# Four DMA transposes of the first tile of chunks 2 and 3 issued ahead of the output stores in a fused attention and GEGLU kernel

## The chip, the cores and the metric

One core of one Trainium2 chip. Times are device microseconds (us) of an execution, given as medians of several. Ratios with a 95% interval compare a kernel with the kernel before in runs that were interleaved on the same chip. The profile's span is some 1.7 us shorter than the time of the same execution (227.4 us of 229.07 us for the kernel before).

## The reference

The input x has 2048 rows of 512 bf16 values. It is normalized, goes through an attention branch and a gated feed-forward branch, and the product of both is added to x:

```python
xn = _layernorm(x, axis=-1)
s = _A_ref(xn, A_wqkv, A_wo)     # 32 heads of 16; each row sees 8 rows, 2 apart; softmax; output projection
g = _silu(_B_ref(xn, B_w_gate, B_w_up, B_w_down))   # (gelu(xn @ w_gate) * (xn @ w_up)) @ w_down, 1792 wide
return x + s * g
```

## The kernel before

The rows are worked on in four chunks of 512 (TQ), each of four tiles of 128 rows (TPQ = 4). For each chunk TensorE does 14 steps of the gate and up projections ("glu"), the QKV projection of the next chunk ("qkv"), the down projection ("down"), the attention sums, and the output projection ("finish"). All of these need the normalized rows transposed, with the 512 features on the partitions. For tiles 6 and 7 of chunk 1 and all of chunks 2 and 3 the transposition is a DMA, four per tile, issued from SyncE's queue, which also issues every other transfer:

```python
    def transpose_by_dma(t, cs=range(NC)):
        j, i = divmod(t, TPQ)
        if i == 0 and 0 in cs:
            xnT[j] = xtp.tile([P, NC, TQ], BF16, name="xnT")      # two buffers
        for c in cs:
            nc.sync.dma_start(
                out=xnT[j][:, c, i * P : (i + 1) * P],
                in_=xns[t][:, c * P : (c + 1) * P],
                transpose=True,
            )

    def project(ps, w, lo, j, i0=0, n=TQ):                        # glu and qkv
        for dk in range(NC):
            nc.tensor.matmul(ps, lhsT=w[:, dk, lo : lo + P],
                rhs=xnT[j][:, dk, i0 : i0 + n], start=(dk == 0), stop=(dk == NC - 1))

    # ... load_v: four loads of v_arr, 520 KB each; sums() ends with load_v(j + 1)

    def finish(j, tt, cols, sl):
        # ... four matmuls into s
        m = sm2.tile([P, n], BF16, name="m")
        nc.vector.tensor_tensor(out=m[:], in0=s[:], in1=sl[:], op=ALU.mult)
        o_t = sm4.tile([P, n], BF16, name="o_t")                  # four buffers
        nc.vector.tensor_tensor(out=o_t[:], in0=m[:], in1=x_sb[:, t, cols], op=ALU.add)
        nc.sync.dma_start(out=out2d[t * P : (t + 1) * P, cols], in_=o_t[:])
```

The order of the program is the order of issue on each engine. Side work is hung on steps of the main loop with `at`, and `run` calls it ahead of the step:

```python
    for i in range(TPQ):
        # ...
        at(("down", 0, 2), normalize, 2 * TPQ + i)
        at(("glu", 1, 0), transpose_by_dma, 2 * TPQ + i)
        # ...
        at(("qkv", 2, i), normalize, 3 * TPQ + i)
        at(("glu", 2, 0), transpose_by_dma, 3 * TPQ + i)
    # ...
    for j in range(NJ):
        for fc in range(NF):
            run("glu", j, fc)
            glu(j, fc)
        if j + 1 < NJ:
            for i, fo in enumerate((0, 1, 4, 5, 2, 3, 6, 7, 8, 9, 10, 11)):
                run("qkv", j + 1, i)
                qkv(j + 1, fo)
            full = slice(0, D)
            sl = []
            for tt in range(TPQ):
                run("down", j, tt)
                sl.append(down(j, tt, full))
                if tt == 0:
                    sums(j)
            divide(j)
            for tt in range(TPQ):
                finish(j, tt, full, sl[tt])
```

So chunk 2's 16 transposes are issued at the start of chunk 1's loop, behind chunk 0's four output stores, and are first read by the QKV projection at the end of that loop; chunk 3's likewise, one chunk later. Chunks are counted from 0.

The softmax here doesn't subtract the row's maximum and nothing guards it: scores larger than these inputs give would overflow.

## Time and profile before

| | before |
|---|---|
| median of the runs at the time of the prediction | 229.31 us (228.83 to 229.8) |
| span of the profile | 227.4 us |
| TensorE busy | 222.3 us (98%) |
| last transpose of chunk 2 issued / first QKV matmul that reads chunk 2 | 96.11 / 98.37 us |
| last transpose of chunk 3 issued / first QKV matmul that reads chunk 3 | 150.16 / 152.23 us |

In the profile PE is TensorE, PEld its loading of weights, DVE VectorE, ACT ScalarE, POOL GpSimd, and SPq the queue from which SyncE issues DMAs. The granted clock is TensorE's clock as the chip allowed it, as a share of full speed. A line of the timeline has a start, a length (both in us), an engine, a source line, an operation with its output and input, and how often it came in a row. The length of a DMA instruction is that of its issue alone. The lines themselves are in the prediction below.

### The profile page before, as it was taken

What the parts mean: (1) busy time and instruction counts of PE and PEld (TensorE: products, weight loads), DVE (VectorE), ACT (ScalarE), POOL (GpSimd) and SP (SyncE); (2) the same over time, 40 slices, a digit from 0 to 9 for tenths busy, and PEclk for the clock granted to TensorE, in tenths of its full rate; (3) what the DMA queues carried; (4) which work ended last, traced back from release to release, by engine and by line L of the source; (5) the groups of instructions that cost most, each with busy time, mean ns of one, the idle gap of its engine ahead of it and who ended that gap; (6) DMA issues with size and microseconds to landing.
All of it is one profiled execution on the core that took longest, in us unless ns stands there. A gap on an engine that the chain in (4) does not pass through costs nothing.

```text
span 227.4 us, 3595 instructions
## 1 busy us (share of the span) xinstructions
PE 222.3 (98%) x1326; PEld 107.1 (47%) x1326; DVE 151.8 (67%) x278; ACT 132.2 (58%) x209; POOL 25.0 (11%) x67
## 2 busy tenths in 40 slices
PE   8999999999999999999999999999999999999993
PEld 4785444444444444444444444444444444444453
DVE  4696981899995588969904759924934348971434
ACT  4279769777531676766751466767763356756210
POOL 1027901000040000333700000000000000000000
PEclk9999999999999999999999999999999999999998
DMA  6999499941039911100219921100217950000011
GB/s 206 349 395 384 127 201 142 321 109 67 28 83 202 223 25 25 29 10 0 92 33 206 214 71 29 26 18 0 81 26 151 197 140 0 0 0 22 12 37 56
DMA packets 30130, 24.64 MB, mean 108 GB/s; under 512 B 10784, under 2 KB 29600, under 8 KB 30112
## 3 DMA queue, kind: packets, MB, share of 16 engines
q1 hardware_dynamic: 30112, 24.41, 44.3%
q8 instruction: 10, 0.16, 0.3%
q14 instruction: 8, 0.07, 0.1%
HBM read 18.74 MB, written 4.34 MB: 102 GB/s over the span
## 4 chain that ended last, share of the span: by engine, by line
PE 95%; DVE 1%; ACT 1%; DMA 1%; issue 0%; DVEq 0%
PE y_ps L443 21%; PE u_ps L249 21%; PE g_ps L249 21%; PE qkv_ps L249 16%; PE s_ps L459 6%; PE L_ps L338 3%; PE o_ps L406 3%; PE qk_ps L554 2%; DMA x_sb<-in_A_x_dram 1%; PE v_ps L554 1%; ACT L431 1%; DVE stats L182 1%; PE tr L214 1%; PE den_ps L358 0%; ACT ge L431 0%; ACT vst L273 0%
## 5 line engine op out<-in xcount | busy, mean ns | idle before, releaser
L249 PE MATMUL u_ps<-xnT,wu_sb 128*128 128x512 bf16 x224 | 57.5, 379 | 0.0
L249 PE MATMUL g_ps<-xnT,wg_sb 128*128 128x512 bf16 x224 | 57.5, 379 | 0.0
L443 PE MATMUL y_ps<-wd_sb,h 128*128 128x512 bf16 (+1 forms) x238 | 49.9, 367 | 0.0
L435 DVE TENSOR_TENSOR h<-ge,u 128x512 bf16<-128x512 bf16 x56 | 23.8, 425 | 30.7 <-ACT u L433 29.0
L433 ACT ACTIVATE u<-u_ps 128x512 bf16<-128x512 f32 x56 | 33.5, 598 | 16.4 <-PE u_ps L249 16.4
L431 ACT ACTIVATE ge<-g_ps 128x512 bf16<-128x512 f32 x56 | 33.5, 598 | 16.2 <-PE g_ps L249 16.0
L320 DVE TENSOR_TENSOR pk<-q_sb,k_sb 128x1024 bf16<-128x1024 bf16 (+1 forms) x56 | 38.9, 762 | 4.6 <-ACT k_sb L273 4.6
L392 DVE TENSOR_TENSOR pv<-E,v_arr 128x1024 bf16<-128x1024 bf16 (+1 forms) x48 | 39.8, 863 | 0.2 <-issue 0.2
L249 PE MATMUL qkv_ps<-xnT,wqkv_sb 128*128 128x512 bf16 (+1 forms) x192 | 37.0, 352 | 0.0
L443 PEld LDWEIGHTS <-h 128*128 128x128 bf16 x238 | 23.0, 98 | 25.9 <-issue 1.3
L249 PEld LDWEIGHTS <-wu_sb 128*128 128x128 bf16 x224 | 21.9, 98 | 26.6 <-issue 0.3
L249 PEld LDWEIGHTS <-wg_sb 128*128 128x128 bf16 x224 | 21.7, 98 | 26.3 <-issue 0.8
L451 ACT ACTIVATE sl<-y_ps 128x512 bf16<-128x512 f32 (+1 forms) x17 | 9.7, 572 | 32.6 <-PE y_ps L443 32.6
L249 PEld LDWEIGHTS <-wqkv_sb 128*128 128x128 bf16 x192 | 18.8, 98 | 17.5
L467 DVE TENSOR_TENSOR m<-s_ps,sl 128x512 bf16<-128x512 f32 (+1 forms) x17 | 11.1, 655 | 17.0 <-PE s_ps L459 17.0
L418 DVE TENSOR_TENSOR oT<-o_ps,rb 128x1024 bf16<-128x1024 f32 x8 | 9.4, 1220 | 13.8 <-DMA rb<-rs_d 13.8
L199 POOL TENSOR_TENSOR rstd<-rstd,mhalf 128x1 f32<-128x1 f32 x12 | 8.0, 663 | 69.9 <-DVE rstd L196 69.9
L459 PE MATMUL s_ps<-wo_sb,oT 128*128 128x512 bf16 (+1 forms) x68 | 14.8, 366 | 0.0
L273 ACT ACTIVATE vst<-qkv_ps 128x512 bf16<-128x512 f32 x14 | 8.4, 597 | 3.7 <-PE qkv_ps L249 3.7
L273 ACT ACTIVATE k_sb<-qkv_ps 128x512 bf16<-128x512 f32 x14 | 8.4, 601 | 3.2 <-PE qkv_ps L249 3.2
L273 ACT ACTIVATE q_sb<-qkv_ps 128x512 bf16<-128x512 f32 x14 | 8.3, 603 | 3.0 <-PE qkv_ps L249 3.0
L459 PEld LDWEIGHTS <-oT 128*128 128x128 bf16 x68 | 6.7, 98 | 7.2
(57 smaller groups left out, 131.4 us busy)
## 6 DMA issues: line engine op xcount, KB each, us to landing
v_arr<-vT SPq DMA_DIRECT2D x16, 520.0 KB, 8.5
vT<-vst SPq DMA_DIRECT2D x8, 256.0 KB, 2.2
out_dram<-o_t SPq DMA_DIRECT2D x15, 128.0 KB, 3.4
wg_sb<-in_B_w_gate_dram SPq DMA_DIRECT2D x2, 896.0 KB, 10.1
wu_sb<-in_B_w_up_dram SPq DMA_DIRECT2D x2, 896.0 KB, 11.0
wd_sb<-in_B_w_down_dram SPq DMA_DIRECT2D x1, 1792.0 KB, 11.5
wqkv_sb<-in_A_wqkv_dram SPq DMA_DIRECT2D x4, 384.0 KB, 4.9
x_sb<-in_A_x_dram SPq DMA_DIRECT2D x3, 512.0 KB, 10.5
```

Source lines behind the costliest of these rows:

```text
L249: nc.tensor.matmul(ps, lhsT=w[:, dk, lo : lo + P], rhs=xnT[j][:, dk, i0 : i0 + n], start=(dk == 0), stop=(dk == NC - 1),)
L273: nc.scalar.activation(out=dst, in_=ps, func=AF.Copy)
L320: nc.vector.tensor_tensor(out=st[j]["pk"][w][:, c0 : c0 + n, :], in0=st[j]["q"][:, c0 : c0 + n, :], in1=k_sb[j][:, c0 : c0 + n, off : off ...
L392: nc.vector.tensor_tensor(out=pv[:, d : d + n, :], in0=st[j]["E"][:, wh, :].unsqueeze(1).to_broadcast([P, n, TQ]), in1=st[j]["va"][:, 4 * ...
L418: nc.vector.tensor_tensor(out=oT[:, g : g + 2, :], in0=st[j]["o"][:, g : g + 2, :], in1=st[j]["rb"][:].unsqueeze(1).to_broadcast([P, 2, TQ ...
L431: nc.scalar.activation(out=ge[:], in_=g_ps[:], func=AF.Gelu_apprx_tanh)
L433: nc.scalar.activation(out=u[:], in_=u_ps[:], func=AF.Copy)
L435: nc.vector.tensor_tensor(out=h[:], in0=ge[:], in1=u[:], op=ALU.mult)
L443: nc.tensor.matmul(y[:], lhsT=st[j][fc][:, tt * P : (tt + 1) * P], rhs=wd_sb[:, fc, cols], start=(fc == 0), stop=(fc == NF - 1),)
L451: nc.scalar.activation(out=sl[:], in_=y[:], func=AF.Silu)
L459: nc.tensor.matmul(s[:], lhsT=st[j]["oT"][:, g, tt * P : (tt + 1) * P], rhs=wo_sb[:, g, cols], start=(g == 0), stop=(g == NC - 1),)
L467: nc.vector.tensor_tensor(out=m[:], in0=s[:], in1=sl[:], op=ALU.mult)
```

## The change

SyncE has nothing to issue for five to six microseconds at the end of chunks 0 and 1, while it waits for the first output tile. The change puts the four transposes of the next-but-one chunk's first tile there:

```diff
-        at(("glu", 1, 0), transpose_by_dma, 2 * TPQ + i)
+        at(("glu", 1, 0) if i else ("down", 0, 3), transpose_by_dma, 2 * TPQ + i)
         at(("glu", 1, 10 + i), moments, 3 * TPQ + i)
         at(("qkv", 2, i), normalize, 3 * TPQ + i)
-        at(("glu", 2, 0), transpose_by_dma, 3 * TPQ + i)
+        at(("glu", 2, 0) if i else ("down", 1, 3), transpose_by_dma, 3 * TPQ + i)
```

## The prediction

> **What bounds the kernel now.** I read the page first (busy shares, then the chain that ended last), then the waits of TensorE, then the waits and the timeline of the DMA queue that SyncE feeds, and last a window of three microseconds around the place where the moved transposes are used.
>
> The page of the kernel before, its busy shares and the engines of its chain:
>
> ```profile
> span 227.4 us, 3595 instructions
> PE 222.3 (98%) x1326; PEld 107.1 (47%) x1326; DVE 151.8 (67%) x278; ACT 132.2 (58%) x209; POOL 25.0 (11%) x67
> ...
> PE 95%; DVE 1%; ACT 1%; DMA 1%; issue 0%; DVEq 0%
> ```
>
> TensorE is busy for 222.3 of 227.4 us, and 95% of the chain is TensorE. The chain in order of time has no piece of another engine between 20.93 us (first matmuls of the feed-forward loop) and 223.91 us (the end): 203 us of matmuls laid end to end. The waits of TensorE agree; this is the whole answer for that engine:
>
> ```profile
> PE warm_ps L231 <- PEq L622: 0.8, 1, 0.8
> PE v_ps L554 <- DVE xnT L225: 0.5, 1, 0.5
> ```
>
> Both lie in the first 7 us. The columns are total wait, times, longest. No matmul waits for a DMA transpose anywhere. Over 74.4 to 98.4, 98.4 to 128.2, 128.2 to 152.2 and 152.2 to 182.1 us, the four stretches that hold the transposes and their first use, the busy time of TensorE equals the length of the stretch (107.70 of 107.70 us) at a granted clock of 1.00. So there is nothing to take away from TensorE's idle time in the stages that the change touches.
>
> The diff touches only the order of SyncE's DMA issues. Its timeline around the ends of chunks 0 and 1 (start, length, line, operation, count):
>
> ```profile
> 65.37 2.64 SPq L294 DMA_DIRECT2D v_arr<-vT  x4
> 73.05 3.52 SPq L470 DMA_DIRECT2D out_dram<-o_t  x4
> 76.62 3.86 SPq L241 DMA_TRANSPOSE xnT<-xn  x3
> ```
>
> ```profile
> 117.97 2.58 SPq L294 DMA_DIRECT2D v_arr<-vT  x4
> 126.91 3.52 SPq L470 DMA_DIRECT2D out_dram<-o_t  x4
> 130.48 20.91 SPq L241 DMA_TRANSPOSE xnT<-xn  x16
> ```
>
> SyncE has nothing to issue from 68.0 to 73.05 us and from 120.55 to 126.91 us: its next instruction is an output store, and the waits of that queue put the longest single waits in these two windows (5.0 and 6.3 us) down to the store's operand o_t from VectorE. Then the stores and all 16 transposes go out, and the last transpose comes late. The timeline between 96.5 and 99.9 us:
>
> ```profile
> 96.11 1.23 SPq L241 DMA_TRANSPOSE xnT<-xn  x1
> ...
> 98.15 1.82 PEld L249 LDWEIGHTS <-wqkv_sb 128*128 128x128 bf16 x9
> 98.37 1.89 PE L249 MATMUL qkv_ps<-xnT,wqkv_sb 128*128 128x512 bf16 x8
> ```
>
> The last of chunk 2's 16 transposes is issued at 96.11 us. From issue to landing a transpose takes 2.3 us in that window (2.2 at least, 4.0 at most, the 4.0 being the first, behind other traffic), so it lands at about 98.4 us. It carries the fourth quarter of the contraction, which the fourth matmul of the first QKV group reads, at 98.37 + 3 x 0.216 = 99.02 us (0.216 is 0.86 us for four matmuls in the chain in order of time). **The slack is about 0.6 us.** For chunk 3 the last issue is at 150.16 us (130.48 + 20.91 - 1.23), landing is near 152.5 us, the first QKV matmul starts at 152.23 us and the fourth at 152.88: slack about 0.4 us. That is narrow, but it is positive in the trace, and this is what the change enlarges.
>
> **What the Trainium skill says.** "Perfetto Trace Analysis", section "DMA Instruction — HWDGE", says that the profiled length of such an instruction ends when the sequencer is free again and leaves out the data movement, and that a semaphore wait lies ahead of its start. The trace agrees: a transpose is 1.23 us long and lands 2.3 us after its start; the idle stretch ahead of the stores is such a wait. "DMA: Bandwidth & Descriptors", section "Rules for kernel authors", advises issuing a DMA early and waiting on it late, which is the intent here, and says a transpose next to ordinary DMAs needs nothing; the order of the changed kernel has indeed no new wait between the kinds except a reused semaphore (below). The same page, section "Queues, rings and completion order", says that each DMA engine takes descriptors in ring order. From this I expect the early transposes to land behind the four v_arr loads that are in flight, not beside them; the 4.0 us of the first transpose at 76.62 us, behind stores that land at 80.4 us, agrees. "Perfetto Trace Analysis", section "Identifying the Most-Contended Engine", warns that matmul busy time says little of the distance from roofline. That holds here too, but the change does not make a matmul shorter.
>
> **The change part by part.** The order of instructions of both kernels differs on SyncE alone; TensorE, VectorE, ScalarE and GpSimd keep theirs. Nothing is added or removed: 4 of 16 transposes of chunk 2, and 4 of chunk 3, go from after the chunk's four output stores to before them.
>
> 1. *What they need is there.* The four normalizes of chunk 2 run on VectorE from 65.85 to 67.22 us, before the load of v_arr has been issued. Those of chunk 3 come at about 100 us. The buffer of xnT that is overwritten was last read at 44.6 and 98.4 us.
>
> 2. *Where they go.* Four transposes at 1.23 to 1.3 us are 4.9 to 5.2 us. They fit almost exactly into 68.0 to 73.05 (5.05 us) and easily into 120.55 to 126.91 (6.36 us). So chunk 2's run from 68.05 to about 73.2, chunk 3's from 120.6 to about 125.7 us, and no first store is late by more than 0.2 us.
>
> 3. *What comes of the stores.* The DMA semaphores go round by eight. In the kernel before, the transposes behind the stores reused those of the four v_arr loads; now the stores do, so store n waits for v_arr load n to land. From the median landing times of windows that hold one or two issues each: chunk 1's loads land at about 70.8, 73.6, 76.2 and 79.1 us (issue plus 5.4, 7.6, 9.6, 11.8), chunk 2's at 123.2, 125.8, 128.4 and 131.0. The stores were issued at 73.05, 74.11, 75.17, 76.24 and at 126.91, 127.97, 129.04, 130.10. So in chunk 0 the third is delayed by some 1.0 us and the fourth by 2.9, in chunk 1 only the fourth, by 0.9. Nobody reads what is stored, and o_t has four buffers whose next use is one chunk (54 us) later: this delay costs nothing.
>
> 4. *What comes of the last transpose.* Chunk 2: the fourth store ends at about 79.5 us, then 12 transposes at 1.25 to 1.3 us take 15.3 us: issue is over at about 95 instead of 97.34 us. Chunk 3: from 131.4 us, over at about 146.8 instead of 151.39. So of the 5.0 us moved, some 2.4 and 4.6 us come off the last landing. The slack grows from 0.6 to about 3 us and from 0.4 to about 5 us.
>
> 5. *What lies on the path.* TensorE's first use is at 98.37 and 152.23 us whatever the transposes do, since it comes right behind the last feed-forward matmul. Taken off the path: 0.00 us in the profiled run. In runs whose DMA is half a microsecond slower, TensorE may stall for a few tenths, twice. The three runs of before lie 228.83 to 229.8 us, so all such effects together are within 1 us; I give the change 0.1 us on average. Sum: 229.31 - 0.1 = 229.2 us.
>
> **The rivals.**
> - *A hidden stall in the unprofiled runs.* If TensorE usually lost about half a microsecond at both chunk borders, the gain would be up to 1.0 us, near 228.3 us. For it: slacks of 0.4 and 0.6 us are thin. Against it: the profiled run took 229.07 us, in the middle of the others, and shows no stall. Even then the gain is 0.4%.
> - *The load of v_arr is slowed by the early transposes.* The first product with v_arr is at 80.61 us and the load lands at 79.1: 1.5 us of room (134.47 against 131.0 in the next chunk). Transposes are 32 KB each, 0.13 MB, which at the 190 GB/s of that window are 0.7 us if they went ahead; behind in the ring they cost none. If they took 3 us, VectorE would slip by 1.5 us, but the last h of the chunk is ready at 99.7 us and used first at 108.7 us, so TensorE would not see it. Time: 229.2 us.
> - *SyncE gets stuck.* If a transpose ahead of the stores waited long (for instance for a semaphore of the rb loads that it now reuses), stores and 12 transposes would slip with it, and each microsecond beyond the slack stalls TensorE. Those loads of 32 KB land in 1.8 us and are needed by the divide at 67.14 and 119.30 us, so they are done. If the fourth store had to wait until 82 us, the twelve would end at 97.3, as now. A loss would need more than that: with 2 us in one chunk 231 us. I give it a few per cent.
> - *The end of the kernel.* The last stores are not moved; nothing changes there.
>
> **How the range and the chances follow.** The work of TensorE is untouched, 203 us without a gap, and the change can win only gaps. Range: the spread of before (228.83 to 229.8), widened by 0.5 us downwards for the first rival and 0.2 us upwards: 228.3 to 230.0 us. Faster by over 2% means below 224.7 us, which would need 4.6 us from gaps that do not exist; slower by over 2% means above 233.9 us and needs a stall of 4 us that nothing points to. One per cent each.
>
> **What the changed profile would show.** TensorE's waits unchanged, still two, in the first 7 us; its start of QKV at 98.4 and 152.2 us unchanged. SyncE's timeline: four transposes at 68 and 120.6 us ahead of the stores, 12 behind, the last issued near 94 and 145.5 us. Waits of the stores with a DMA of v_arr as the releaser for the last one or two stores of chunk 0: that shows step 3. If the twelve still end near 97 us, step 4 is wrong, and the idle time was not there to be had. The prediction as a whole would be wrong if a matmul waited for xnT in the changed kernel, or if the time moved by over 1 us with the same gapless TensorE.

## The result, and the profile after

The kernel after took 228.95 us (median of 6 runs, 228.81 to 229.35), the kernel before 229.41 us in the same rounds (228.83 to 229.8). The ratio is 0.9986 with a 95% interval of 0.9968 to 1.0003. A ratio is the mean time of one kernel's runs over that of the other's of the same rounds, so it is not quite the ratio of the medians. The class is "same".

SyncE's timeline around the ends of chunks 0 and 1, kernel after:

```profile
65.50 2.62 SPq L294 DMA_DIRECT2D v_arr<-vT  x4
68.22 5.08 SPq L241 DMA_TRANSPOSE xnT<-xn  x4
73.40 6.42 SPq L470 DMA_DIRECT2D out_dram<-o_t  x4
79.88 15.40 SPq L241 DMA_TRANSPOSE xnT<-xn  x12
...
118.17 2.65 SPq L294 DMA_DIRECT2D v_arr<-vT  x4
120.86 5.13 SPq L241 DMA_TRANSPOSE xnT<-xn  x4
127.04 5.01 SPq L470 DMA_DIRECT2D out_dram<-o_t  x4
132.10 15.98 SPq L241 DMA_TRANSPOSE xnT<-xn  x12
```

The four transposes fill the idle time, as intended. The stores behind them now take 6.42 and 5.01 us to go out instead of 3.52. The queue's own waits, kernel after, say what for (the queue and line that waited, the releaser, then total us, times, longest); first 60 to 90 us, then 115 to 140 us:

```profile
SPq L470 <- DMA v_arr<-vT: 4.4, 2, 2.5
...
SPq L470 <- DMA v_arr<-vT: 2.4, 2, 2.2
```

Two stores in each place wait for a v_arr load to land. A wait counts from the end of the instruction before, so it is not the delay of the store. The delay is read from the start of the fourth store in each place:

```profile
79.49 0.33 SPq L470 DMA_DIRECT2D out_dram<-o_t  x1
...
131.72 0.33 SPq L470 DMA_DIRECT2D out_dram<-o_t  x1
```

These are 3.25 and 1.62 us later than in the kernel before (76.24 and 130.10 us), and each comes right after the landing of the fourth v_arr load, at 79.4 us (67.44 + 12.0) and 131.6 us (120.13 + 11.5). The last transpose is issued 1.23 us ahead of the end of its row, so at 94.05 us instead of 96.11, and at 146.85 us instead of 150.16. TensorE takes no notice. Its waits in the kernel after, all of them:

```profile
PE warm_ps L231 <- PEq L622: 0.8, 1, 0.8
PE v_ps L554 <- DVE xnT L225: 0.5, 1, 0.5
```

They are the two of before, number for number. The chain in order of time shows where the 0.1 us between the two spans (227.4 and 227.5 us) lies; its QKV pieces are first those of the kernel before, then those of the kernel after:

```profile
12.61 5.25 PE qkv_ps L249 x48
44.62 10.36 PE qkv_ps L249 x48
98.53 10.36 PE qkv_ps L249 x48
152.39 10.36 PE qkv_ps L249 x48
```

```profile
12.75 5.25 PE qkv_ps L249 x48
44.76 10.36 PE qkv_ps L249 x48
98.66 10.36 PE qkv_ps L249 x48
152.52 10.36 PE qkv_ps L249 x48
```

The kernel after is 0.14 us later at the first of these pieces, before anything that the change touches, and 0.13 us later at the last. From the first piece to the end of the span it is 214.79 us before (227.4 - 12.61) and 214.75 us after (227.5 - 12.75).

### The profile page after: what moved, and what is told of

It is laid out like the page before. It is cut to its first block, busy times and chain, and to the rows that moved or that the text cites. A ratio compares the mean times of both kernels' runs of the same rounds, so it can differ in the third digit from the quotient of the medians.

```text
span 227.5 us, 3601 instructions
## 1 busy us (share of the span) xinstructions
PE 222.6 (98%) x1326; PEld 107.6 (47%) x1326; DVE 151.6 (67%) x278; ACT 132.1 (58%) x209; POOL 18.9 (8%) x67
## 4 chain that ended last, share of the span: by engine, by line
PE 97%; ACT 1%; DVE 0%; issue 0%; DVEq 0%
PE y_ps L443 21%; PE u_ps L249 21%; PE g_ps L249 21%; PE qkv_ps L249 16%; PE s_ps L459 6%; PE L_ps L338 3%; PE o_ps L406 3%; PE qk_ps L554 2%; PE warm_ps L231 1%; PE v_ps L554 1%; PE qk_ps L529 1%; ACT L431 1%; PE tr L214 1%; PE den_ps L358 0%; PE v_ps L529 0%; ACT ge L431 0%
## 6 DMA issues: line engine op xcount, KB each, us to landing
wd_sb<-in_B_w_down_dram SPq DMA_DIRECT2D x1, 1792.0 KB, 11.6
```

## The experiments

Ten kernels were run, in three calls, each call on one chip with its own runs of the kernel before. All ten gave correct results.

| kernel | median us | before, same call | ratio | 95% interval |
|---|---|---|---|---|
| a_again: the change once more | 229.29 | 229.25 | 1.0002 | 0.9983 to 1.0021 |
| c2_only: chunk 2 alone | 229.44 | 229.04 | 1.0011 | 0.9996 to 1.0026 |
| c3_only: chunk 3 alone | 229.27 | 229.04 | 1.0010 | 0.9991 to 1.0030 |
| all16: all 16 transposes first | 229.12 | 229.04 | 1.0005 | 0.9989 to 1.0020 |
| b_extra1: before, one redundant transpose per chunk | 231.40 | 229.24 | 1.0094 | 1.0075 to 1.0114 |
| b_extra2: before, two | 234.00 | 229.25 | 1.0201 | 1.0177 to 1.0225 |
| b_extra4: before, four | 243.34 | 229.04 | 1.0621 | 1.0604 to 1.0637 |
| a_extra2: after, two | 229.09 | 229.25 | 0.9994 | 0.9975 to 1.0012 |
| a_extra4: after, four | 233.54 | 229.25 | 1.0183 | 1.0154 to 1.0213 |
| all16_extra4: all 16 first, four | 229.32 | 229.24 | 1.0000 | 0.9984 to 1.0016 |

### Is there a gain at all? The change again, and each half

a_again is the changed kernel unaltered. The halves each keep one of the two changed lines:

```diff
 c2_only
-        at(("glu", 1, 0), transpose_by_dma, 2 * TPQ + i)
+        at(("glu", 1, 0) if i else ("down", 0, 3), transpose_by_dma, 2 * TPQ + i)
 c3_only
-        at(("glu", 2, 0), transpose_by_dma, 3 * TPQ + i)
+        at(("glu", 2, 0) if i else ("down", 1, 3), transpose_by_dma, 3 * TPQ + i)
```

> The changed kernel once more, in five rounds, to narrow the interval of its ratio to the kernel before. Theory (TensorE is gapless at both places in both kernels, nothing to win): ratio 1.000 within 0.15%. Rival (the kernel before loses up to 0.5 us at each of two chunk borders in runs that were not profiled): ratio 0.996 to 0.998 with an interval that leaves out 1.

> The change for chunk 2 alone. Theory (no gain anywhere): ratio 1.000. Rival (a small true gain at each border): ratio 0.999, half of the change's.

> The change for chunk 3 alone, whose slack is the smaller one (0.4 us). Theory (no gain anywhere): ratio 1.000. Rival (a small true gain at each border, the larger where the slack is smaller): ratio 0.998 to 0.999.

None of the three differs from the kernel before; the 0.14% of the first comparison did not come back. A gain of some 0.1% is not excluded by intervals of 0.15 to 0.2% to either side, but the larger hidden stall, 0.4%, is: it lies outside a_again's interval (0.9983 and up). One profile does show a small stall of this kind. In c2_only, whose chunk 3 keeps the old order, the 48 QKV matmuls of chunk 3 take 10.45 us from the first start to the start of the down projection (152.43 to 162.88 us); in both places of the kernels before, after and c3_only, and in chunk 2 of c2_only, they take 10.36 us. So the old order lost 0.09 us there, far less than the 0.5 us of the rival.

### How much room do the transposes have? Redundant transposes

Slack is the time between the landing of the last transpose and the moment at which TensorE needs it. The test of slack is to use it up. These kernels repeat one, two or all four transposes of the second tile, same source and same destination, between the third tile's and the last tile's. The data stay right; the last landing gets later by about 1.27 us for each. The edit to the kernel before, with n = 2 (one redundant transpose is `range(1, 2)`, four are `range(4)`), is the same for the kernel after:

```diff
         at(("glu", 1, 0), transpose_by_dma, 2 * TPQ + i)
+        if i == 2:
+            at(("glu", 1, 0), transpose_by_dma, 2 * TPQ + 1, range(2))
 ...
         at(("glu", 2, 0), transpose_by_dma, 3 * TPQ + i)
+        if i == 2:
+            at(("glu", 2, 0), transpose_by_dma, 3 * TPQ + 1, range(2))
```

**One and two on the kernel before.**

> The kernel before with one redundant transpose (1.27 us of issue) ahead of the last tile's four in chunks 2 and 3. It reads the slack of the kernel before in unprofiled runs, as so short a wait should leave the clock alone. Slack as predicted (0.6 and 0.4 us): waits of 0.65 and 0.85 us, time up by 1.5 us, ratio 1.0065. Slack as thin as the run with two redundant transposes suggests (about 0.15 us each): 2.2 us, ratio 1.0098. No slack and a hidden stall in usual runs: 2.5 us, ratio 1.011.

> The kernel before with two redundant transposes (second tile, same data, same place) ahead of the last tile's four, in chunks 2 and 3. Each costs about 1.26 us of issue, so the last landing is 2.5 us later. Theory (slack of 0.6 us in chunk 2 and 0.4 us in chunk 3, no hidden stall): TensorE waits 1.9 and 2.1 us for xnT, time up by 4.0 us, ratio 1.0175. Rival (slack already used up in usual runs): the whole 5.0 us, ratio 1.022. Second rival (a stall of TensorE is made up for later): ratio 1.00 to 1.01.

One transpose in each place costs 231.40 - 229.24 = 2.16 us. It adds 2.54 us of issue in all, so 0.38 us were free, or **0.2 us at each place on average**, less than half of what the prediction read from one trace. The interval of the ratio (1.0075 to 1.0114) allows 0 to 0.4 us at each place, which leaves out the predicted average of 0.5 but not zero. The waits of TensorE in the profile of b_extra1 name the cause:

```profile
PE qkv_ps L249 <- DMA xnT<-xn: 1.4, 2, 0.7
PE v_ps L558 <- DMA wqkv_sb<-in_A_wqkv_dram: 0.9, 1, 0.9
```

The profile has two more waits, those of the kernel before. The second line here is a wait for weights at the start of the kernel, ahead of all these transposes: the first QKV piece of the chain starts at 14.00 us here and at 12.61 us in the kernel before. This profiled run is the slowest of its six (232.18 us), and its span is 3.1 us above that of the kernel before, of which 1.4 us are this late start. The first line counts gaps between busy stretches as modelled, so from the timeline of TensorE in b_extra1 the stalls are read as starts:

```profile
99.76 0.81 PE L249 MATMUL qkv_ps<-xnT,wqkv_sb 128*128 128x512 bf16 x3
101.29 9.01 PE L249 MATMUL qkv_ps<-xnT,wqkv_sb 128*128 128x512 bf16 x40 [0.72 <-DMA xnT<-xn]
```

Three QKV matmuls run, and the fourth, the one that reads the last quarter, starts at 101.29 us instead of 99.76 + 0.65 = 100.41: 0.88 us late. In chunk 3 it is 155.97 against 154.49 + 0.65, 0.83 us. In this profile the slack was therefore 1.27 - 0.88 = 0.39 and 0.44 us. Where the kernel before keeps its order, other profiles give other values: in c3_only chunk 2's last transpose is issued at 96.80 us, lands 2.3 us later at 99.10, and is needed at 98.71 + 0.65 = 99.36, slack 0.26; in c2_only chunk 3's is issued at 150.74, lands 2.4 us later at 153.14, needed at 152.43 + 0.65 = 153.08, so no slack is left within the accuracy of these numbers (this is the place of the 0.09 us stall above). In these traces the slack of the order before lies between 0 and 0.6 us. Part of the spread is the issue of the fourth store: single lines of the timeline, kernel b_extra2, give

```profile
75.64 0.33 SPq L470 DMA_DIRECT2D out_dram<-o_t  x1
76.70 0.92 SPq L470 DMA_DIRECT2D out_dram<-o_t  x1
```

The fourth took 0.92 us, the third 0.33, and in the kernel before the fourth also took 0.33. All transposes behind it start 0.6 us later. The queue's waits show no longer wait for this store than in the kernel before; why its issue takes longer stays open.

Two transposes in each place cost 234.00 - 229.25 = 4.75 us, between the 4.0 us of the theory and the 5.0 us of the first rival. From the profile, stalls of 101.94 - 98.84 - 0.65 = 2.45 us in chunk 2 and 159.59 - 156.83 - 0.65 = 2.11 us in chunk 3 make 4.6 us. But the span of this profile is 234.0 us, 6.6 more than before. The windows of b_extra2 show the rest (from:to in us, length, busy times of PE, PEld, DVE, ACT and POOL with counts, then the granted clock of TensorE, DMA share, GB/s):

```profile
98.84:101.94 3.10, 1.13 (x4) 0.29 (x3) 2.24 (x8) 0.60 (x1) 0.74 (x2) 1.00 0.11 24
101.94:105.00 3.06, 3.06 (x8) 1.10 (x8) 0.00 (x0) 1.19 (x2) 0.00 (x0) 0.55 0.02 5
105.00:108.00 3.00, 3.00 (x14) 1.34 (x13) 0.74 (x2) 1.70 (x3) 0.00 (x0) 0.89 0.00 0
108.00:113.34 5.34, 5.29 (x26) 2.38 (x26) 5.34 (x10) 3.67 (x7) 0.25 (x1) 1.00 0.00 0
```

In the first window TensorE is busy for 1.13 of 3.10 us, waiting for transposes. Right after, **the granted clock is 0.55** for 3 us, then 0.89, then full. The 45 remaining QKV matmuls (the trace lacks the record of one) took 113.34 - 101.94 = 11.4 us where 45 x 0.216 = 9.7 us is their usual pace: the stall of 2.45 us cost another 1.7. In chunk 3 of the same profile, after a stall of 2.11 us, the clock stayed at 1.00 and they took 9.7 us (159.59 to 169.30). Another 0.5 us of this span is a later start of the first QKV piece (13.08 against 12.61 us). The four other runs of this kernel have spans of 231.5 to 232.7 us, near the 227.4 + 4.6 = 232.0 us without such a dip.

**Four on the kernel before.**

> The kernel before with four redundant transposes ahead of the last tile's four in chunks 2 and 3: 5.0 us of issue in each. Theory (slack 0.6 and 0.4 us): waits of TensorE of 4.4 and 4.6 us, time up by 9.0 us, ratio 1.039. Rival (TensorE makes up part of a longer stall, or falls to a lower clock after it): clearly less or clearly more than 5.0 us above the kernel with two redundant transposes.

The theory's 9.0 us were too few: it took 14.3 us more (243.34 - 229.04). The first QKV matmul would have been due at 98.73 and 159.07 us (0.86 us after the start of the last up projection); the fourth, due 0.65 us after that, started at 104.35 and 164.95. The stalls are 4.97 and 5.23 us, since the slack was nearly nil in this profile and, in chunk 3, the transposes went out every 1.32 us (twenty in 26.44 us). The clock fell at both:

```profile
104.35:108.00 3.65, 3.65 (x10) 1.39 (x11) 0.00 (x0) 1.19 (x2) 0.00 (x0) 0.58 0.02 4
165.00:170.00 5.00, 5.00 (x15) 1.86 (x15) 0.00 (x0) 1.92 (x4) 0.00 (x0) 0.61 0.00 0
```

The clock is 0.58 and 0.61 right after the stalls (in chunk 3 it fell already during the stall, 0.75 from 159.07 to 164.95 us). The 45 remaining matmuls took 115.58 - 104.35 = 11.2 and 176.58 - 164.95 = 11.6 us instead of 9.7, so the dips cost 1.5 and 1.9 us. In the four runs the mean granted clock is 0.971 to 0.977, against 0.997 to 1.000 in the kernel before, so here the dip came every time. The second rival was the right one: these longer stalls cost more than their length. That the stalls bring the dips is supported by all twelve profiles: in steps of 3 us, no other stretch of any of them has a clock below 1.00 until the last matmul.

**Two and four on the kernel after.**

> The changed kernel with the same two redundant transposes in chunks 2 and 3. Theory (the change widened the slack to 2.8 us in chunk 2 and 3.7 us in chunk 3): 2.5 us fit, no wait of TensorE, ratio to the kernel before 0.998 to 1.000. Rival (the slack did not grow, since stores and later transposes slipped): 4 us more, ratio 1.0175.

> The changed kernel with four redundant transposes in chunks 2 and 3, 5.0 us of issue in each. Theory: slack 2.8 and 3.7 us, so waits of 2.2 and 1.3 us, time up by 3.5 us, ratio to the kernel before 1.014. Rival (slack grew by the full 5 us of the four moved transposes, to 5.6 and 5.4 us): no wait, ratio 1.000. Other rival (no growth of the slack): 9 us, ratio 1.039.

This is where the two kernels differ. The two redundant transposes that cost the kernel before 2.0% cost the kernel after nothing, and its profile has no wait of TensorE for xnT. With four it stalls, and its timeline gives the slack that the change made:

```profile
98.10 0.86 PE L249 MATMUL qkv_ps<-xnT,wqkv_sb 128*128 128x512 bf16 x2
99.84 0.39 PE L249 MATMUL qkv_ps<-xnT,wqkv_sb 128*128 128x512 bf16 x1 [0.89 <-DMA xnT<-xn]
101.09 9.89 PE L249 MATMUL qkv_ps<-xnT,wqkv_sb 128*128 128x512 bf16 x44 [0.86 <-DMA xnT<-xn]
...
154.31 0.94 PE L249 MATMUL qkv_ps<-xnT,wqkv_sb 128*128 128x512 bf16 x3
156.17 9.87 PE L249 MATMUL qkv_ps<-xnT,wqkv_sb 128*128 128x512 bf16 x44 [0.91 <-DMA xnT<-xn]
```

In chunk 2 the fourth QKV matmul starts at 101.09 us instead of 98.10 + 0.65 = 98.75, so 2.34 us late, and in chunk 3 156.17 instead of 154.31 + 0.65 = 154.96, 1.21 us. Four transposes are 5.08 us, so the slack is 5.08 - 2.34 = 2.7 us and 5.08 - 1.21 = 3.9 us. Both stalls together, 3.55 us, agree with that profile's span: 230.7 - 227.4 = 3.3 us. The median of the runs is 4.3 us above before, more than the theory's 3.5 us; the interval of the ratio (1.0154 to 1.0213) leaves out its 1.014. The clock stayed at 1.00 after both stalls of this profile. Two of the other five runs have a mean clock of 0.991 and 0.993, as low as the profiled run of b_extra2 with its one dip (0.993), so dips there are likely but not shown; another run took 234.08 us at a clock of 1.000, and the rest is not taken apart.

### What becomes of the stores, and how far can the idea be taken? All 16 first

```diff
-        at(("glu", 1, 0), transpose_by_dma, 2 * TPQ + i)
+        at(("down", 0, 3), transpose_by_dma, 2 * TPQ + i)
 ...
-        at(("glu", 2, 0), transpose_by_dma, 3 * TPQ + i)
+        at(("down", 1, 3), transpose_by_dma, 3 * TPQ + i)
```

> All 16 transposes of chunks 2 and 3 ahead of the four output stores, instead of 4. Theory (nothing on the path, stores have time): ratio 0.998 to 1.000, same as the change; the second tile's transposes now wait for the landing of the v_arr loads, whose semaphores they reuse, and the stores no longer do; last transpose issued near 90 and 143 us, slack near 8 us in both. Rival (the late stores hold up something, or hold VectorE through o_t): a wait of VectorE on o_t, ratio above 1.005.

The ratio is 1.0005, as the theory has it. SyncE's timeline at the end of chunk 0 and its waits from 66 to 99 us, kernel all16:

```profile
68.25 22.97 SPq L241 DMA_TRANSPOSE xnT<-xn  x16
91.32 1.99 SPq L470 DMA_DIRECT2D out_dram<-o_t  x4
```

```profile
SPq L241 <- DMA v_arr<-vT: 2.3, 2, 1.7
```

The wait for v_arr has moved from the stores to the transposes that now come fifth to eighth and reuse the semaphores of the v_arr loads (the seventh goes out at 76.44 us and the eighth at 79.65 us, as the third and fourth load land); no store waits for v_arr any more. That confirms that the stores' waits in the changed kernel come with the order of issue and not with the store. The last transpose is issued at 68.25 + 22.97 - 1.23 = 89.99 us and, one chunk later, at 140.95 us (120.22 + 21.96 - 1.23): 6 and 9 us earlier than before. The stores go out at 91.3 us, 18 us later than before, and VectorE does not wait for their buffer.

all16_extra4 adds the four redundant transposes to that order, with the edit of the extra kernels hung on the same two steps as the transposes.

> All 16 transposes and the four redundant ones of chunks 2 and 3 ahead of the output stores. Theory (slack of about 7 and 10 us with all 16 first): 5.0 us fit, no wait of TensorE, ratio to the kernel before 1.000, where four redundant ones cost the kernel before 6.2% and the changed kernel 1.8%. Rival (late stores or the shared DMA queue take the room back): a wait of TensorE for xnT, ratio above 1.01.

Its ratio is 1.0000, and its profile has no wait of TensorE for xnT. The same added work of four transposes per chunk costs 6.2% in the order before, 1.8% in the changed order and nothing with all 16 first. None of these orders is faster than the kernel before as long as nothing is added, and no run points to one that would be by more than the 0.1% that these intervals cannot resolve.

## Why the prediction was right or wrong

The prediction said 229.2 us with 98% for "same"; 228.95 us came, inside its range. Its steps:

1. **The data are there and the transposes go into the idle time.** Right. They run from 68.22 to 73.30 and from 120.86 to 125.99 us; predicted were 68.05 to 73.2 and 120.6 to 125.7. That they would land behind the v_arr loads in flight was right too: the first, issued at 68.22 us, lands 11.6 us later at 79.8, just behind the fourth load at 79.4 us.
2. **The stores inherit the waits for v_arr.** Right in kind, as the waits of the kernel after and all16 show. In chunk 0 the third store goes out 1.4 us and the fourth 3.25 us later than in the kernel before (predicted 1.0 and 2.9). In chunk 1 the fourth is 1.6 us later (predicted 0.9) and the third only by the 0.13 us by which the whole profile is later, as predicted; the second wait of 0.2 us there delays nothing. The 0.7 us too little come mostly from the fourth v_arr load, which was issued 0.2 us later in this run and landed at 131.6 us instead of the assumed 131.0.
3. **The last transpose comes earlier by 2.4 and 4.6 us.** The end of the issue moved from 97.34 to 95.28 us, 2.1 us, and from 151.39 to 148.08 us, 3.3 us. The second was mis-sized by 1.3 us: 0.6 of it from the later stores (132.05 against 131.4), the rest from twelve transposes in 15.98 instead of 15.3 us.
4. **The slack grows.** Right in direction. Predicted were 3 and 5 us after the change; a_extra4 measures 2.7 and 3.9. The slack before was mis-sized: 0.6 and 0.4 us were read from one trace, and b_extra1 puts it at 0.2 us on average over unprofiled runs, 0 to 0.6 over the traces. One trace gives one value of a difference between the times of two engines, and the prediction did not allow for that.
5. **Nothing comes off the path.** Right. TensorE's waits, the start of its QKV matmuls relative to the first piece of the chain, and its clock are those of before. The 0.1 us that the prediction gave the change on average was neither shown nor excluded.

Of the rivals, the *hidden stall* worth up to 1.0 us was not found: the change again gave 1.0002, and each half 1.001. With a slack that sometimes is nil, a small stall does happen in the old order (0.09 us in c2_only's chunk 3), and a few tenths of a microsecond in some runs remain possible and could not be resolved. The *slowed v_arr load* did not hold anything up: the first product with v_arr starts at 80.74 us in the kernel after and 80.61 us before, which is the 0.13 us by which the whole profile is later. *SyncE gets stuck* did not happen, but its price was put too low: the prediction took each microsecond beyond the slack as one microsecond of time, while b_extra2 and b_extra4 show 1.5 to 1.9 us on top per stall when the clock falls.

## What to carry to other kernels

A queue's idle time is worth something only if an engine on the path waits for what the queue issues later; here TensorE had no gap to give back, and the reordering bought room, 2.1 and 3.3 us of it by the time of the last issue, without a gain in time that could be measured. Measure such room by using it up with redundant work of known length, since one trace shows one value of a slack that varied by 0.6 us. Before an issue is moved ahead, look at which semaphores change hands: the stores here took over waits on loads with which they share no data.

## What the Trainium skill lacked or had wrong

- "TensorE: Matmul & The Clock Gate", section "Why this matters for your kernels", advises no idle gaps of more than about 3 us between bursts of matmuls. Here a stretch with several shorter gaps was enough: in b_extra2 TensorE was busy for 1.13 of 3.10 us, with no single gap above 1 us by the timeline (0.98 and 0.86), and the granted clock then was 0.55 for 3 us, at a cost of 1.7 us. In chunk 3 of the same profile gaps of 0.84 and 0.88 us left the clock at 1.00, and so did a nearly equal stretch of a_extra4 (busy for 1.14 of 2.99 us, gaps of 0.89 and 0.86). So the length of a single gap, which this advice goes by, was not a safe limit here, and the dip is not certain below it either.
- "Advanced Engine Details and Errata", section "X-Bar Transpose (TRN2)", says that transpose DMAs are as fast as regular DMAs. For small ones issued in a row that is not so here: a transpose of 128 x 128 bf16 (32 KB) takes 1.23 us to issue and one goes out every 1.27 us, some 26 GB/s, while a 128 KB store takes 0.33 us to issue. It is SyncE's issue, not the movement of the data, that fills the queue's time: from 84 to 96 us in the kernel before the DMA engines are busy for 0.12 of it. The landing itself, 2.3 us after the start, is near that of the plain 32 KB loads of rb (1.8 us).
- No page that we read says that moving a DMA's issue can hand semaphores, which the program reuses in turn, from one later DMA to another. Here output stores came to wait 4.4 and 2.4 us for loads with which they share no data.
